# Two operand spacings in SBUF, for a fused attention and SwiGLU kernel: block words of h and the weights of 320 tokens

## The chip, the cores and the metric

One core of a Trainium2 chip runs the kernel. The metric is the device time of one execution in microseconds, lower is better. Before the change it is 702.36 us, the median of three runs (702.23 to 702.74).

## The reference

Attention is done in two steps through 32 packing tokens: the packing tokens p attend to k and v, and the queries then attend to what came out. The result, 4608 tokens by 512, goes through a gated feed-forward layer (512 to 1536 and back).

```python
def sm_attn(qq, kk, vv):
    s = scale * np.matmul(qq, kk.transpose(0, 1, 3, 2))
    a = np.exp(s - np.max(s, axis=-1, keepdims=True))
    a = a / (np.sum(a, axis=-1, keepdims=True) + 1e-09)
    return np.matmul(a, vv)
p_packed = sm_attn(p, k, v)              # 8 batches, 8 heads, 32 tokens, 64
out = sm_attn(q, p_packed, p_packed)     # 8 batches, 8 heads, 576 tokens, 64
x = out, as 4608 tokens by 512
g = x @ w_gate
return (g / (1 + np.exp(-g)) * (x @ w_val)) @ w_out
```

## The kernel before

Every float32 operand of a large product is split into two words, a high one that TensorE takes as it is and a low one that holds the rest, and a product is three matmuls: low by high, high by low, high by high.

The attention never forms its output. For each batch, m is the gate and value weights times the packed tokens (line 361, `m_mm`), and the gate and value of a chunk of h are m times the attention weights `a2` (line 1538 for batches 2 to 7, line 924 for batch 1, line 1104 for batch 0). In line 1538 the stationary operand is 128 columns of m and the moving one is `a2`, 320 tokens in a batch's first phase and 256 in its second. Each phase has 12 chunks, each chunk two sums (gate, value) and each sum six matmuls, so twelve matmuls of one width follow each other. ScalarE makes silu of the gate, VectorE multiplies (line 1552).

h times w_out goes by Strassen-like blocks (lines 1397 to 1407, `products`). GpSimd makes sums of h's blocks (`pair_sums`), and `pair_words` casts seven blocks of 128 columns to high words on ScalarE (line 1362) and takes the low words on VectorE (line 1363). In line 1404 these block words are stationary; the words of w_out or of sums of its blocks (`wo_h`, `wo_l`, `tA`, `tB`) are moving, 256 columns. A half of a pair has three block products, nine matmuls, the other half four, twelve matmuls.

`words_room` hands out two sets of rooms in turn. A set is a room for seven high words and one for seven low words, 896 elements of 4 bytes each. The first set lies in the second room of the ring `a2` (`x`), the second in a room called `pair9` (`y`) and behind the sums in `tB` (`z`):

```python
sums["set"] = ((x[:, 16:912], x[:, 1040:1936]), (y[:, 16:912], z[:, 16:912]))
```

All engines' queues follow orders written out by hand (`PROGRAM`, `FIRST`, `LATER` and the loops). `ROOMS` lists the SBUF rooms in the order in which they are laid out; sizes are rounded up to 32 bytes. Before the change the rooms of w_out's words, `tA`, `tB` and both rooms of `a2` start at 96 bytes modulo 256. The block words start 16 elements, 64 bytes, into rooms of that kind, so at 160. The rooms of m are at 160 as well: `mh` and `ml` start there, and those in `io0` and `io1` begin 16 elements in. All steps inside these operands that one matmul or the next takes are multiples of 256 bytes, or of 512 for stationary ones. So in lines 1538, 1404, 946, 924 and 1104 the stationary operand is 64 bytes (modulo 256) above the moving one throughout.

Of the kernel before, what the change touches and what calls it, by code (L numbers as in the profile page):

```python
# [11 lines left out]
F32R = mybir.dt.float32r  # L12
# [8 lines left out]
B, H, S, D = 8, 8, 576, 64  # L21
NP = 32
DM, DF = 512, 1536
P = 128
NPAR, NHP = 2, 4
NFC = DF // P
# [8 lines left out]
NA, NB = 256, 320  # L35
PART = slice(0, NA), slice(NA, NA + NB)
NZ = NA // P
PHASE = NB, NA
NT = B * S
SCALE = 1.0 / 8.0  # L40
POSITIVE_MOST = float(np.array(0x0FEFFFFF, np.int32).view(np.float32))
# [1 line left out]
LOW_WORD = 2.0**-29 * 15 / 16  # L43

ROOMS = (
    ("p", 512, 2), ("pp", 512, 1), ("ppt", 512, 2), ("z1", 64, 2),
    ("t2", 2560, 1), ("sg", 1280, 1), ("s2", 5120, 1), ("a1", 5120, 1), ("wA", 24576, 1), ("wB", 8192, 1), ("wC", 16384, 1),
    ("io0", 9216, 2), ("io1", 9216, 2), ("v", 10240, 1), *((f"pair{i}", 4096, 1) for i in range(NFC + 1)), ("a2", 9216, 2),
    ("t4", 6144, 1), ("hc", 8192, 1), ("nm1", 16, 2), ("hw", 6144, 1), ("ot", 5120, 1), ("x1", 256, 1), ("r2", 432, 1), ("mx1", 16, 2), ("mh", 4096, 2), ("ml", 4096, 2),
)  # L50

PROGRAM = """
# [108 lines left out]
def tile_pack_attention_swiglu(ctx: ExitStack, tc: tile.TileContext, q0, qT, qP, kT, kP, v, vq, pT, wgv, wout, out):  # L161
# [5 lines left out]
    pool = ctx.enter_context(tc.tile_pool(name="pool", bufs=1))  # L167
# [74 lines left out]
    rings, turns = {}, {}  # L242
# [62 lines left out]
    kps, vs, qs, st1, st2, a2, ppts = {}, {}, {}, {}, {}, {}, {}  # L305

    def piece(n):
        if "kqv" not in rings:
            rings["kqv"] = pool.tile([P, 2, 1280], F32, tag="v", bufs=1, name="kqv")
        return rings["kqv"][:, ring("kqv", 2), :n]  # L310
# [14 lines left out]
    def load_qp(b, i):  # L325
        n, at = PHASE[i], i * PHASE[0]
        x = piece(NHP * n)
        nc.sync.dma_start(x, qP[b - NEARLY, :, NHP * at : NHP * (at + n)])
        qs.setdefault(b, []).append(x.rearrange("p (h n) -> p h n", h=NHP))
# [272 lines left out]
    def s2_tiles(b):  # L602
        st2[b] = (
            pool.tile([P, 2, NPAR, HS] if b == 1 else [P, NPAR, S], F32, tag="s2", bufs=1, name="s2"),
            pool.tile([P, 3, 2 * NPAR * NBK], F32, tag="r2", bufs=1, name="r2"),
        )
# [172 lines left out]
    def y_tiles(b):  # L779
        s2_tiles(b)  # L780
        if "a2" not in rings:
            rings["a2"] = pool.tile([P, 2 * NPAR * S], F32R, tag="a2", bufs=2, name="a2")
        a2[b] = [
            [
                rings["a2"][:, at : at + NPAR * n].rearrange("p (r n) -> p r n", r=NPAR)
                for at in (2 * NPAR * PHASE[0] * i, 2 * NPAR * PHASE[0] * i + NPAR * n)
            ]
            for i, n in enumerate(PHASE)
        ]
# [9 lines left out]
    def y_flat(b, i):  # L799

        at = NPAR * PHASE[0]
        return st2[b][0].rearrange("p r n -> p (r n)")[:, slice(0, at) if i == 0 else slice(at, NPAR * S)]

    def y_view(b, i):

        n = PHASE[i]
        x = y_flat(b, i).rearrange("p (k n) -> p k n", n=NP)
        rows = slice(0, NPAR * PHASE[0] // NP) if i == 0 else slice(NPAR * PHASE[0] // NP, NPAR * S // NP)
        return x, [st2[b][1][:, j, rows] for j in range(3)], [P, NPAR * n // NP, NP]
# [89 lines left out]
    t4 = {}  # L899
# [54 lines left out]
    def emit_out(acc, row, eng):  # L954
# [21 lines left out]
        "pack": q_pack,  # L976
        "flip": q_flip,
        "tiles": y_tiles,
    }

# [22 lines left out]
    with tc.manual_schedule(engines={mybir.EngineType.PE}):  # L1003
# [17 lines left out]
        with tc.manual_schedule(  # L1021
# [190 lines left out]
            for word in PROGRAM.split():  # L1212
                name = word[: word.index(":") + 1] if ":" in word else word.rstrip("0123456789")
# [125 lines left out]
        sums = {"pairs": 0, "words": 0}  # L1339

        def words_room():

            i = sums["words"] % 2
            sums["words"] += 1
            if "set" not in sums:
                x = pool.tile([P, 2304], F32R, tag="a2", bufs=2, name="hw0")
                y = pool.tile([P, 1024], F32R, tag="pair9", bufs=1, name="hw1")
                z = t_tiles["B"][:, 3072:]
                sums["set"] = ((x[:, 16:912], x[:, 1040:1936]), (y[:, 16:912], z[:, 16:912]))
            return [x.rearrange("p (i n) -> p i n", n=P) for x in sums["set"][i]]  # L1350

        def pair_sums(x, eng=nc.gpsimd):
# [7 lines left out]
        def pair_words(x):  # L1360
            hi, lo = words_room()
            nc.scalar.copy(hi, x[:, 1:])  # L1362
            nc.vector.tensor_tensor(lo, x[:, 1:], hi.bitcast(F32), op=ALU.subtract)  # L1363
            return dict(zip(WORDS, ((hi[:, i], lo[:, i]) for i in range(7))))
# [14 lines left out]
        def rest_words(k, a22, tb, s):  # L1379

            hi, lo = words_room()
            srcs = ((slice(0, 2), tb[:, 2 * k : 2 * k + 2]), (2, a22), (slice(3, 7), s))
            for at, src in srcs:
                nc.scalar.copy(hi[:, at], src)
            for at, src in srcs:
                nc.vector.tensor_tensor(lo[:, at], src, hi[:, at].bitcast(F32), op=ALU.subtract)
            return dict(zip(("A11", "A12", "A22", *WORDS[3:]), ((hi[:, i], lo[:, i]) for i in range(7))))
# [127 lines left out]
        with tc.manual_schedule(  # L1515
# [3 lines left out]
            for b in range(2, B):  # L1519
                plan = plan_of(b)  # L1520
                for slot in range(2 * NFC):
                    ph, fc = divmod(slot, NFC)
                    k, f = divmod(fc, 2)
                    n, odd = PHASE[ph], b % 2
# [25 lines left out]
                    x = rings["hc"][:, sums["pairs"] % 2]  # L1550
# [106 lines left out]
```

## Time and profile before

| what | value |
|---|---|
| median of three runs | 702.36 us (702.23 to 702.74) |
| profiled execution | 702.56 us |
| its span, first to last instruction | 700.6 us |
| instructions | 16313 |
| TensorE busy | 694.6 us, 99% of the span |
| weight loads busy | 608.3 us, 87% |
| VectorE busy | 506.7 us, 72% |

The profiled execution is 2.0 us longer than its span: what lies around the first and the last instruction. Matmuls overlap in the profile (the next starts before the one ahead of it is recorded as ended), so a busy share of TensorE says little; the spacing from one start to the next does. The chain of work that ended last gives that: it is cut into pieces of one line, and a piece's length is the time from its start to the start of the next piece.

### The profile page before, as it was taken

The page shows a single profiled execution, that of the slowest core. Times are in us where ns is not written, and L with a number is a line of the kernel's source. Part 1 is how long each engine was busy: PE and PEld are TensorE (multiplying, and loading weights), DVE is VectorE, ACT ScalarE, POOL GpSimd, SP SyncE. Part 2 cuts the span into 40 slices and gives each one's busy share as a digit, 9 for nine tenths or more (in the row PEclk, how much of TensorE's full clock was granted, in tenths as well). Part 3 has the DMA queues.
Part 4 walks back from the last instruction along what each step waited for, and adds up shares of the span by engine and source line. Part 5 has one row for each costly group of instructions (what it writes and reads, how often), then busy time and mean ns, then how long its engine had stood idle before and what let it go on. Part 6 is the DMA issues. An engine that isn't in the chain of part 4 may idle for free.

```text
span 700.6 us, 16313 instructions
## 1 busy us (share of the span) xinstructions
PE 694.6 (99%) x6623; PEld 608.3 (87%) x6623; DVE 506.7 (72%) x1032; ACT 399.9 (57%) x670; POOL 167.2 (24%) x283
## 2 busy tenths in 40 slices
PE   9999999999999999999999999999999999999998
PEld 7777787887788988999988998899888998889997
DVE  4997997567886687757897559766687559753854
ACT  3999874655765457463375546745375546533432
POOL 0000005035162222123032222221231222223221
PEclk9999999999999999999999999999999999999999
DMA  9999942134263354513244416342544414320000
GB/s 348 363 341 342 356 183 99 45 107 151 71 229 109 112 167 150 192 64 133 82 165 139 154 69 219 127 162 64 185 156 142 153 69 155 107 109 1 31 31 31
DMA packets 27354, 103.53 MB, mean 148 GB/s; under 512 B 6800, under 2 KB 8336, under 8 KB 20112
## 3 DMA queue, kind: packets, MB, share of 16 engines
q1 hardware_dynamic: 26992, 102.30, 41.4%
q8 instruction: 52, 0.85, 0.5%
q10 hardware_dynamic: 288, 0.20, 0.1%
q14 instruction: 22, 0.18, 0.1%
HBM read 86.57 MB, written 15.91 MB: 146 GB/s over the span
## 4 chain that ended last, share of the span: by engine, by line
PE 88%; DMA 1%; DVE 0%; issue 0%
PE gv L1538 33%; PE acc L1404 30%; PE acc L946 8%; PE aux L361 8%; PE gv L924 5%; PE gv L1104 2%; PE aux L503 1%; PE aux L586 1%; DMA q_t<-in_qT 1%; PE end L1478 0%; DVE wo_f L227 0%; DVE ot L1487 0%; PE aux L598 0%; DVE wo_l L303 0%; DVE wo_f L226 0%; DVE hw L1137 0%
## 5 line engine op out<-in xcount | busy, mean ns | idle before, releaser
L1538 PE MATMUL gv<-a,m 128*128 128x320 f32 (+1 forms) x1728 | 251.0, 294 | 0.0
L1538 PEld LDWEIGHTS gv<-a,m 128*128 128x128 f32 x1728 | 232.0, 188 | 3.2 <-issue 2.3
L1548 ACT ACTIVATE sg<-gv 128x320 f32<-128x320 f32 (+1 forms) x144 | 59.3, 412 | 171.7 <-PE gv L1538 150.4
L1354 POOL TENSOR_TENSOR hc<-hc 128x256 f32<-128x256 f32 x69 | 51.1, 740 | 346.7 <-DVE hc L1552 346.7
L1552 DVE TENSOR_TENSOR hc<-gv,sg 128x256 f32<-128x256 f32 x144 | 60.3, 419 | 93.6 <-PE gv L1538 81.6
L1404 PE MATMUL acc<-wo_h,hw 128*128 128x256 f32 x500 | 125.6, 282 | 0.0
L1404 PEld LDWEIGHTS acc<-wo_h,hw 128*128 128x128 f32 x500 | 90.8, 188 | 11.0 <-issue 4.2
L1404 PE MATMUL acc<-wo_l,hw 128*128 128x256 f32 x332 | 92.5, 278 | 0.0
L1404 PE MATMUL acc<-tA,hw 128*128 128x256 f32 x420 | 75.0, 278 | 0.0
L1362 ACT CAST hw<-hc 128x896 fp32r<-128x896 f32 x71 | 66.5, 936 | 7.1 <-DVE hc L1358 3.9
L946 PE MATMUL acc<-wo_h,hw 128*128 128x512 f32 x192 | 69.7, 408 | 0.0
L1404 PEld LDWEIGHTS acc<-wo_l,hw 128*128 128x128 f32 x332 | 62.5, 188 | 0.0
L1404 PEld LDWEIGHTS acc<-tA,hw 128*128 128x128 f32 x420 | 60.8, 188 | 0.0
L946 PEld LDWEIGHTS acc<-wo_h,hw 128*128 128x128 f32 x192 | 36.1, 188 | 19.7 <-issue 11.3
L891 ACT CAST m<-aux 128x512 fp32r<-128x512 f32 x72 | 38.8, 592 | 23.1 <-PE aux L361 22.8
L849 DVE TENSOR_TENSOR m<-aux,m 128x512 fp32r<-128x512 f32 x72 | 46.0, 680 | 4.1 <-ACT m L891 4.0
L1404 PE MATMUL acc<-wo_h,tB 128*128 128x256 f32 x164 | 46.2, 282 | 0.0
L1363 DVE TENSOR_TENSOR hw<-hc,hw 128x896 fp32r<-128x896 f32 x36 | 39.3, 1091 | 7.0 <-ACT hw L1362 6.5
L1363 DVE TENSOR_TENSOR tB<-hc,hw 128x896 fp32r<-128x896 f32 x35 | 38.5, 1099 | 4.9 <-ACT hw L1362 4.5
L361 PE MATMUL aux<-wB,ppt 64*32 64x512 f32 x608 | 41.8, 601 | 0.0
L946 PE MATMUL acc<-wo_l,hw 128*128 128x512 f32 x96 | 38.0, 396 | 0.0
L1404 PE MATMUL acc<-tB,hw 128*128 128x256 f32 x204 | 36.8, 282 | 0.0
(240 smaller groups left out, 1195.7 us busy)
## 6 DMA issues: line engine op xcount, KB each, us to landing
wB<-wd SPq DMA_DIRECT2D x36, 1024.0 KB, 4.9
st<-in_wgv SPq DMA_DIRECT2D x12, 1024.0 KB, 7.9
out<-ot SPq DMA_DIRECT2D x33, 256.0 KB, 2.5
kqv<-in_vq SPq DMA_DIRECT2D x12, 640.0 KB, 4.1
kqv<-in_kP SPq DMA_DIRECT2D x12, 576.0 KB, 3.8
st<-in_wout SPq DMA_DIRECT2D x6, 1024.0 KB, 7.2
kqv<-in_qP SPq DMA_DIRECT2D x6, 640.0 KB, 4.5
wd<-wA SPq DMA_DIRECT2D x3, 1024.0 KB, 11.0
```

The source lines that it names most:

```text
L361: nc.tensor.matmul(outs[par][32 * hp : 32 * hp + 32], lhs(r, hp), rhs(r, hp), start=True, stop=True)
L849: pin(nc.vector.tensor_tensor(*lows.pop(0), op=ALU.subtract))
L891: nc.scalar.copy(m[0][at], src)
L924: nc.tensor.matmul(pg[:, :n], m_[:, g, f, s * P : (s + 1) * P], a_[:, g, off : off + n], start=(i == 0), stop=(i == 5),)
L946: nc.tensor.matmul(acc[:, :], h_[:, c : c + P], w_[fc // 2][:, fc % 2], start=(first and i == 0), stop=(fc == NFC - 1 and i == 2),)
L1354: eng.tensor_tensor(x[:, 4:6], x[:, 0].unsqueeze(1).broadcast_to([P, 2, P]), x[:, 1:3], op=ALU.subtract)
L1362: nc.scalar.copy(hi, x[:, 1:])
L1363: nc.vector.tensor_tensor(lo, x[:, 1:], hi.bitcast(F32), op=ALU.subtract)
L1404: nc.tensor.matmul(banks[bank][:, 256 * half : 256 * half + 256], s_, m_, start=(start and k == 0 and j == 0), stop=(k == last and j == 2 ...
L1538: nc.tensor.matmul(pg[:, :n], m_[:, g, f, s * P : (s + 1) * P], a_[:, g, :], start=(i == 0), stop=(i == 5))
L1548: nc.scalar.activation(sg[:, :n], pgs[0][:, :n], AF.Silu)
L1552: nc.vector.tensor_tensor(x[:, 2 * f : 2 * f + 2].rearrange("p i n -> p (i n)"), pgs[1][:, o : o + 256], sg[:, o : o + 256], op=ALU.mult,)
```

## The change

The two rooms of `a2` get 16 bytes more each (rounded up to 32), and inside the first, the weights of the 256 tokens come first and those of the 320 tokens behind them with a gap of 4 elements, 16 bytes. The list entry `nm1` (two rooms of 32 bytes) moves from behind `hc` to the front, so that everything from `t2` to `hc` starts 64 bytes later, and the 64 bytes that `a2` has grown by do the same for everything from `hw` on. The four rooms of block words start at other elements of the same tiles.

After it, modulo 256: w_out's words, `tA`, `tB` and the first room of `a2` at 160, m at 224. The 320 tokens' weights are at 176, 48 below m; the 256 tokens' at 160, 64 below m as before. The second room of `a2` starts at 192. The block words are at 32 (high) and 96 (low) above w_out's words in the first set and at 128 (high) and 160 (low) in the second.

```diff
+A2_AT = 2 * NPAR * NA + 4, 0
...
 ROOMS = (
-    ("p", 512, 2), ("pp", 512, 1), ("ppt", 512, 2), ("z1", 64, 2),
+    ("p", 512, 2), ("pp", 512, 1), ("ppt", 512, 2), ("z1", 64, 2), ("nm1", 16, 2),
...
-    ("io0", 9216, 2), ("io1", 9216, 2), ("v", 10240, 1), *((f"pair{i}", 4096, 1) for i in range(NFC + 1)), ("a2", 9216, 2),
-    ("t4", 6144, 1), ("hc", 8192, 1), ("nm1", 16, 2), ("hw", 6144, 1), ("ot", 5120, 1), ("x1", 256, 1), ("r2", 432, 1), ("mx1", 16, 2), ("mh", 4096, 2), ("ml", 4096, 2),
+    ("io0", 9216, 2), ("io1", 9216, 2), ("v", 10240, 1), *((f"pair{i}", 4096, 1) for i in range(NFC + 1)), ("a2", 9232, 2),
+    ("t4", 6144, 1), ("hc", 8192, 1), ("hw", 6144, 1), ("ot", 5120, 1), ("x1", 256, 1), ("r2", 432, 1), ("mx1", 16, 2), ("mh", 4096, 2), ("ml", 4096, 2),
...
-            rings["a2"] = pool.tile([P, 2 * NPAR * S], F32R, tag="a2", bufs=2, name="a2")
+            rings["a2"] = pool.tile([P, 2 * NPAR * S + 4], F32R, tag="a2", bufs=2, name="a2")
...
-                for at in (2 * NPAR * PHASE[0] * i, 2 * NPAR * PHASE[0] * i + NPAR * n)
+                for at in (A2_AT[i], A2_AT[i] + NPAR * n)
...
-                sums["set"] = ((x[:, 16:912], x[:, 1040:1936]), (y[:, 16:912], z[:, 16:912]))
+                sums["set"] = ((x[:, 0:896], x[:, 1040:1936]), (y[:, 32:928], z[:, 40:936]))
```

## Rows read from the trace of the kernel before

**Rows 1.** The page's first part: engine, busy us, share of the span, instructions.
```profile
span 700.6 us, 16313 instructions
PE 694.6 (99%) x6623; PEld 608.3 (87%) x6623; DVE 506.7 (72%) x1032; ACT 399.9 (57%) x670; POOL 167.2 (24%) x283
```
**Rows 2.** The page's chain that ended last: shares by engine and by line.
```profile
PE 88%; DMA 1%; DVE 0%; issue 0%
PE gv L1538 33%; PE acc L1404 30%; PE acc L946 8%; PE aux L361 8%; PE gv L924 5%; PE gv L1104 2%; PE aux L503 1%; PE aux L586 1%; DMA q_t<-in_qT 1%; PE end L1478 0%; DVE wo_f L227 0%; DVE ot L1487 0%; PE aux L598 0%; DVE wo_l L303 0%; DVE wo_f L226 0%; DVE hw L1137 0%
```
**Rows 3.** Waits of the weight loads: waiting line, releaser, us in total, times, longest.
```profile
PEld acc L1404 <- DVE tB L1363: 4.2, 5, 0.8
```
**Rows 4.** The chain in order, 198 to 300 us: start us, us, line, matmuls.
```profile
213.32 1.75 PE gv L1538 x12
215.08 1.37 PE acc L1404 x12
218.20 1.03 PE acc L1404 x9
...
228.15 1.41 PE acc L1404 x12
...
231.32 1.06 PE acc L1404 x9
...
245.16 1.36 PE gv L1538 x12
...
247.22 1.57 PE acc L1404 x12
...
250.15 1.02 PE aux L361 x16
...
272.99 1.62 PE acc L1404 x12
274.61 1.41 PE gv L1538 x12
```
**Rows 5.** The chain in order, 600 us to the end.
```profile
604.39 1.36 PE gv L1538 x12
...
622.93 1.37 PE acc L1404 x12
...
626.06 1.03 PE acc L1404 x9
...
643.46 1.76 PE gv L1538 x12
...
654.40 14.84 PE acc L1404 x126
...
686.62 1.06 PE acc L1404 x9
...
689.09 1.41 PE acc L1404 x12
690.51 1.41 PE gv L1538 x12
```
**Rows 6.** The chain over the whole span, among its longest pieces.
```profile
327.79 14.70 PE acc L1404 x126
```
**Rows 7.** Timeline, 300 to 303 us: start us, us, engine, line, matmuls or loads.
```profile
302.34 0.28 PE L1404 MATMUL acc<-wo_h,hw 128*128 128x256 f32 x1
302.34 0.73 PEld L1538 LDWEIGHTS gv<-a,m 128*128 128x128 f32 x5
302.45 0.74 PE L1538 MATMUL gv<-a,m 128*128 128x320 f32 x4
```
**Rows 8.** Groups by line and shape: busy us, mean ns of one.
```profile
L1538 PE MATMUL gv<-a,m 128*128 128x320 f32 x864 | 138.5, 309 | 0.0
```
**Rows 9.** Line 1404 alone over the span: busy us and instructions, granted clock.
```profile
0.00:700.60 700.60, 230.58 (x1743) 213.68 (x1743) 1.00 0.42 148
```

## The prediction

> **What bounds the kernel now.** I read the first part of the page first: TensorE is busy 694.6 us of a 700.6 us span, and the next engine, VectorE, has 72% [rows 1]. Then the chain that ended last: 88% of it is TensorE, two thirds of that the two lines that the change touches, the gate and value products (line 1538) and the products with w_out (line 1404) [rows 2]. Then the waits in front of the weight loads: the largest releaser with a name, VectorE's line 1363, costs 4.2 us in the whole run, so nobody keeps TensorE waiting for long [rows 3]. What is left to gain or lose is the spacing of back-to-back matmuls, so I read the chain's pieces (how long 9, 12 or more matmuls of one line took, from their first to the next piece's first).
>
> The pieces come in two levels. Twelve matmuls of 256 columns take 1.36 us in one place and 1.41 us in another, nine take 1.02 or 1.06 us: 113.3 or 117.5 ns for one [rows 4, 5]. Line 1538 and line 1404 share these levels, and a level, once there, lasts over several pieces: from 646 us to the end nearly every piece of 256 columns is at 1.41 or 1.06 [rows 5]. Of the pieces of twelve without a start-up in line 1404, 29 are at 1.36 or 1.37 and 16 at 1.41 or 1.42; of nine, 22 at 1.02 or 1.03 and 20 at 1.05 or 1.06; in line 1538 with 256 columns, 38 at 1.36 and 22 at 1.41 or 1.42. With 320 columns there is no such choice: all 68 separate pieces of twelve, first to last, are at 1.75 or 1.76 us, 146.5 ns for one [rows 4, 5]. At the quick level's time per column they would take 1.36 x 320/256 = 1.70 us. The bytes read are alike in all of them, and the operands stand 64 bytes apart (modulo 256) everywhere; so one spacing of the operands allows both levels, and the trace holds no other spacing for these two lines.
>
> Why spacing could matter at all is seen in the timeline: the weight load of a matmul starts as the matmul before it starts (302.34 us for both), so stationary words of the next and moving words of the present one are fetched from SBUF at the same time [rows 7].
>
> **The change part by part.** No instruction, transfer, wait or queue position is added, removed or moved, so no engine's count changes and SP's queue stays as it is. Two spacings change on purpose, (a) and (b), and two more with them, (c).
>
> (a) The 320-token weights: 864 matmuls, 72 groups of twelve [rows 8]. Their moving operand now ends up 48 bytes (modulo 256) below the stationary one, 64 before. No row has this spacing, so the price has to be bounded. Below: they come to the quick level, 72 x (1.757 - 1.70) = 4.1 us gained. Above: they lose one more step of the size that separates the two levels, 146.5 x 117.5/113.3 = 151.9 ns, 864 x 5.4 ns = 4.7 us lost. The nearest rows are the two levels of the 256 columns [rows 4, 5]: there 64 bytes allow the quick level, while with 320 columns they never do, whichever level the pieces in front have (215.08 to 231.32 us has both). A loss that is there in all of 68 pieces is of the kind that a fixed spacing can cause, and I take the lower end: 4.1 us gained.
>
> (b) The block words of h: 1743 matmuls of 256 columns [rows 9], 64 bytes from w_out's before, then 32 and 96 in one set, 128 and 160 in the other. Bounds again from the two levels. If every piece went to the quick level: 16 x 0.05 + 20 x 0.04 for the plain pieces, 6 x 0.04 for pieces of twelve with a start-up (1.61 or 1.62, against 1.57 or 1.58 of 16 others), and 14.70 + 14.84 - 2 x 126 x 0.1133 = 0.99 for the two runs of 126: 2.8 us gained [rows 4 to 6]. Since the level carries over into line 1538's 256-column groups, whose own spacing stays at 64, these would follow: 22 x 0.05, 1.1 us more. If every piece went to the slow level: 29 x 0.05 + 22 x 0.04 + 16 x 0.04 + 0.14 = 3.1 us lost, and 38 x 0.05 = 1.9 us with line 1538. A level worse than 1.41 is not excluded; one more step of 4.2 ns would be 7.3 us on 1743 matmuls. Four different spacings will hardly all be good or all be bad, and at one spacing both levels occur already. So I take the middle, nothing, and keep both ends.
>
> (c) The rooms move as a whole by 64 bytes against the few that stay below them (p, ppt, z1). This shifts the stationary ppt against the gate and value words in line 361, which is 8% of the chain, 56 us [rows 2]. One level step of 3.7% there would be 2.1 us to either side. The 32 pieces in which its 16 matmuls stand alone and entire take 1.02 us each [rows 4], so it shows no second level: nothing. The second room of a2 ends up 32 bytes further on than the rest, so batch 1's weights, which lie there, come to 32 bytes from the words of line 924, 64 before; that line is 5% of the chain, 35 us, and a step 1.3 us. Nothing again, as in (b), and 3.4 us to either side for both.
>
> (d) VectorE, ScalarE and GpSimd read and write the same shapes at other addresses. VectorE, the busiest of them, has 28% idle time [rows 1], which would cover a step of 4%; without that cover it would show as longer waits of the weight loads, now 4.2 us behind line 1363 [rows 3]. A quicker TensorE meets these waits a little sooner; a few tenths of a us.
>
> Sum: 4.1 us off 702.56 us, the time of the profiled execution (span 700.6 and 2.0 around it), is 698.5 us; against the median of 702.36 us, 0.2 lower, it is 698.3 us.
>
> The Trainium skill speaks against all of this (SBUF — State Buffer, "SBUF: two separate sides"): among engines only the port pair that VectorE and GpSimd share makes anyone wait, and TensorE has ports of its own for moving and stationary operands. By that rule the sum is zero, 702.4 us. The trace agrees so far as no row names another engine as the cause of the two levels, but it shows two levels, which the rule doesn't explain; so it stays a rival, below. The skill's gap of N / 2.4 + 2.5 ns (TensorE: Matmul & The Clock Gate, "Back-to-back issue gap") would give 109.2 ns for 256 columns and 135.8 ns for 320; no stretch of this trace reaches either.
>
> **The rivals.**
> R1, no difference: the two levels come from when a group starts, not from where its operands stand. For it: one spacing shows both levels, and a level persists across lines with different tiles [rows 4, 5]. Against it: the 320s never leave theirs. Time 702.4 us.
>
> R2, slower: the new spacings of the block words are worse than 64. One of every three stationary loads in line 1404 takes low words and two take high words, so a bad spacing in one room touches a sixth or a third of 1743 matmuls; all rooms at the slow level and line 1538 with them cost 3.1 + 1.9 = 5.0 us. With the 320s unchanged and the products alone slow: 705.5 us. It decides against my forecast when the products lose more than the 4.1 us of (a): 2.4 ns a matmul, over half of the step of 4.2 ns. For it: 64 already keeps more than half of the pieces at the quick level, so a blind move has more to lose than to win.
>
> R3, both gain: the 320s at 1.70, all else at 1.36 and 1.02: 4.1 + 2.8 + 1.1 = 8.0 us, 694.4 us. For it: products behind a 320-column group are at 1.37 where they are quick, not 1.36 [rows 4, 5], and a quick 320 would hand on a quick start. Against it: level changes also follow the stalls at line 361, which stay.
>
> R4, the gain of (a) and a loss in (b) of 3.1 us nearly cancel: 701.4 us.
>
> **How the numbers follow.** Forecast 0.36 (own range 696.2 to 700.4, the 2.1 us of line 361), R3 0.13, R1 0.17, R2 0.27, R4 0.07. A measurement of this kernel tells 0.2%, 1.4 us, from no change. Faster: forecast and R3, with a hundredth of R1: 0.50. Same: R1 and most of R4: 0.22. Slower: R2 and a hundredth of R4: 0.28. For 8 in 10 the range reaches from below R3, 693.0 us, to 706.5 us, which is R2 with half of what line 1538 can add; what loses both ways, up to 702.4 + 5.0 + 4.7 = 712.1 us, stays outside.
>
> **What the next profile would show.** (a) is right if the 320-column pieces of twelve stand near 1.70 us, and wrong at 1.75 or above. (b) is right if pieces of 1.36 and 1.41 are about as many as now; R2 shows as pieces at 1.41 or more where both words come from one set, with the other set quick; R3 as no 1.41 left. (c) is right if line 361's pieces stay at 1.02. R1 shows as the same levels in the same proportion. Wrong altogether would be a change in instruction counts, in the granted clock, now 1.00 [rows 9], or a new releaser of the weight loads.

## The result, and the profile after

The change made the kernel slower: 710.64 us against 702.30 us (four runs each, 710.11 to 711.82 against 702.05 to 702.74), a ratio of 1.0117 (interval 1.0102 to 1.0132). The profiled execution took 711.82 us, with a span of 709.8 us, 9.2 us more than before.

The first part of the page (engine, busy us, share of the span, instructions), and the chain's shares by engine:

```profile
span 709.8 us, 16313 instructions
PE 703.0 (99%) x6623; PEld 616.6 (87%) x6623; DVE 507.2 (71%) x1032; ACT 398.7 (56%) x670; POOL 166.8 (23%) x283
...
PE 95%; DMA 2%; DVE 1%; ACT 1%; issue 0%; SPq 0%; ACTq 0%; DVEq 0%
```

Every count is as in [rows 1]; TensorE and its weight loads each have some 8 us more, the other engines are within 1.2 us of before. So TensorE's own instructions became longer, at the same granted clock. Line 1404, now 1405, alone over the span (busy and instructions of matmuls, then of weight loads; then the granted clock):

```profile
0.00:709.80 709.80, 234.18 (x1743) 217.20 (x1743) 1.00 0.42 146
```

Against [rows 9] that is 3.6 us more for the same 1743 matmuls. The waits of the weight loads have not grown: the largest with a name is still 4.2 us, as in [rows 3] (as many times and as long, put down to another of VectorE's instructions):

```profile
PEld acc L1405 <- DVE a L843: 4.2, 5, 0.8
```

The chain in order of time, 198 to 300 us (start us, us, line, matmuls; all lines of the kernel are one higher than before):

```profile
217.90 1.76 PE gv L1539 x12
219.66 1.06 PE acc L1405 x9
220.73 1.83 PE gv L1539 x12
222.55 1.42 PE acc L1405 x12
223.97 1.83 PE gv L1539 x12
225.80 1.02 PE aux L362 x16
...
245.99 1.07 PE acc L1405 x9
247.05 1.41 PE gv L1539 x12
...
249.16 1.61 PE acc L1405 x12
...
254.46 1.38 PE gv L1539 x12
```

And 600 us to the end:

```profile
643.42 1.83 PE gv L1539 x12
645.25 1.42 PE acc L1405 x12
...
655.63 1.37 PE gv L1539 x12
657.00 1.42 PE acc L1405 x12
...
663.69 14.88 PE acc L1405 x126
```

Three things differ from [rows 4, 5]. The products (line 1405) have lost the quick level: from 198 us on, 44 pieces of twelve stand at 1.41 or 1.42 and none at 1.36, 46 of nine at 1.06 or 1.07 and none at 1.02. The 256-column groups of line 1539 stand mostly at 1.41 or 1.42, 53 of 62, where it was 22 of 62. And the 320-column groups, which had one level, now have two: 33 pieces at 1.75 or 1.76 and 35 at 1.82 or 1.83. The pieces of line 362 still take 1.02 us.

Where the 9.2 us went follows from each matmul's interval to the start of the next one, summed by line and width in both traces:

| line before, columns | change, us |
|---|---|
| 1404, 256 | +3.5 |
| 1538, 320 | +2.7 |
| 1538, 256 | +1.9 |
| 361, 512 | +0.6 |
| 924, 256 | +0.6 |
| all else, no row more than 0.4 either way | -0.1 |

### The profile page after: what moved, and what is told of

Its sections match the earlier page's. It is cut to its first block, busy times and chain, and to the rows that moved or that the text cites. A ratio compares the mean times of both kernels' runs of the same rounds, so it can differ in the third digit from the quotient of the medians.

```text
span 709.8 us, 16313 instructions
## 1 busy us (share of the span) xinstructions
PE 703.0 (99%) x6623; PEld 616.6 (87%) x6623; DVE 507.2 (71%) x1032; ACT 398.7 (56%) x670; POOL 166.8 (23%) x283
## 4 chain that ended last, share of the span: by engine, by line
PE 95%; DMA 2%; DVE 1%; ACT 1%; issue 0%; SPq 0%; ACTq 0%; DVEq 0%
PE gv L1539 32%; PE acc L1405 30%; PE acc L947 9%; PE aux L362 8%; PE gv L925 5%; PE gv L1105 5%; DMA st<-in_wgv 1%; PE aux L587 1%; PE aux L504 1%; DMA k_t<-in_kT 1%; DMA out<-ot 1%; PE warm_ps L1009 1%; PE end L1479 0%; PE acc_aux L684 0%; PE aux L444 0%; PE acc_aux L362 0%
## 5 line engine op out<-in xcount | busy, mean ns | idle before, releaser
L1539 PE MATMUL gv<-a,m 128*128 128x320 f32 (+1 forms) x1728 | 255.5, 297 | 0.2 <-ACT sg L1549 0.2
L1539 PEld LDWEIGHTS gv<-a,m 128*128 128x128 f32 x1728 | 236.1, 189 | 3.4 <-issue 2.3
```

The source lines that it names most:

```text
L1539: nc.tensor.matmul(pg[:, :n], m_[:, g, f, s * P : (s + 1) * P], a_[:, g, :], start=(i == 0), stop=(i == 5))
```

## The experiments

Three questions were open: which edit costs what; whether the spacing of the two operands decides, or where one of them starts, or how a group begins; and which spacings are good. "Spacing" is the stationary operand's address minus the moving one's, modulo 256, throughout. Each kernel was compared with the kernel before in runs on the same chip.

**words_only**: the kernel before with the block words alone moved, to spacings 32, 96, 128 and 160.

```diff
-                sums["set"] = ((x[:, 16:912], x[:, 1040:1936]), (y[:, 16:912], z[:, 16:912]))
+                sums["set"] = ((x[:, 8:904], x[:, 1048:1944]), (y[:, 32:928], z[:, 40:936]))
```

> Of the change only the block words move: 32 and 96 bytes (modulo 256) from w_out's words in the first set, 128 and 160 in the second; attention weights and all rooms stay as before. Theory A (the spacing of a matmul's stationary operand from its moving one sets its pace): line 1404 loses its quick level as it did in the changed kernel, 3.5 us, and line 1538's 256 columns lose it with them, 1.9 us; the 320 columns stay at 1.76 us for twelve: 707.7 us, 5.4 over 702.3. Theory B (the levels come from when groups start, and the spacing does not matter): 702.3 us, pieces of 1.36 and 1.41 in the old proportion. Theory C (the rooms' 64-byte shift against p, ppt and z1 did it): 702.3 us as well.

Measured: 707.78 us against 701.85, ratio 1.0091 (1.0077 to 1.0105). Its chain from 400 to 440 us, and below it its line 1404 alone over the span:

```profile
401.39 1.76 PE gv L1538 x12
403.15 1.42 PE acc L1404 x12
...
406.33 1.06 PE acc L1404 x9
...
420.23 1.36 PE gv L1538 x12
...
428.91 1.42 PE acc L1404 x12
```
```profile
0.00:705.70 705.70, 234.20 (x1743) 216.97 (x1743) 1.00 0.42 147
```

The products lose all that they lose in the full change (234.20 us busy against 234.18). By intervals line 1404 costs 3.6 us and line 1538's 256-column groups, none of whose addresses moved, 1.7 us: a slow level is handed on. The 320-column pieces keep 1.76.

**weights_only**: all of the change except the words, which go back to a spacing of 64.

```diff
-                sums["set"] = ((x[:, 0:896], x[:, 1040:1936]), (y[:, 32:928], z[:, 40:936]))
+                sums["set"] = ((x[:, 8:904], x[:, 1032:1928]), (y[:, 16:912], z[:, 16:912]))
```

> All of the change but the block words, which stay 64 bytes from w_out's words. Theory A: the 320-token weights at 48 bytes lose 2.7 us as in the changed kernel, line 924 at 32 bytes 0.6 us, line 361 0.6 us, and line 1404 keeps both its levels: 706.2 us, 3.9 over 702.3; line 1538's 256 columns keep pieces of 1.36. If words and weights add, this and the words-only run make 8.3 to 9.3 us together. Theory B: 702.3 us. Theory C: nearly the whole loss is here, above 708 us, and line 1404 is slow although its spacing is 64.

Measured: 705.97 us against 701.85, ratio 1.0055 (1.0043 to 1.0068). Its chain from 400 to 440 us, and its groups by line and shape (busy us, mean ns of one):

```profile
400.37 1.83 PE gv L1539 x12
402.20 1.37 PE acc L1405 x12
403.57 1.83 PE gv L1539 x12
...
437.77 1.02 PE acc L1405 x9
```
```profile
L1539 PE MATMUL gv<-a,m 128*128 128x320 f32 x864 | 143.7, 315 | 0.0
```

The 320-column matmuls took 138.5 us before [rows 8] and take 143.7 here. By intervals that is 5.1 us lost: 745 of 842 stand at 153 to 154 ns, from one start to the next. The products, at 64 again, gain 2.0 us and the 256-column groups 0.9, since nearly all of them are quick here.

**rooms_only** and **rooms_32**: the kernel before with a gap of 64, or of 32, bytes ahead of `t2`. With 64 the stationary `ppt` moves against line 361's words as it does in the change; with 32 all large operands move together by half of that. All other spacings stay.

```diff
-    ("p", 512, 2), ("pp", 512, 1), ("ppt", 512, 2), ("z1", 64, 2),
+    ("p", 512, 2), ("pp", 512, 1), ("ppt", 512, 2), ("z1", 64, 2), ("gap", 64, 1),
```

> Only a gap of 64 bytes in front of t2: every room behind z1 starts 64 bytes later, so all spacings stay but those of ppt and p to the gate and value words and to k and q (lines 361 and 503). Theory A: line 361 may lose up to 0.6 us, nothing else moves: 702.3 to 702.9 us. Theory B: 702.3 us. Theory C: 706 us or more, with line 1404 and line 1538 at the slow level.

> The kernel before with a gap of 32 bytes in front of t2: all spacings of lines 1404 and 1538 stay at 64, but each moving operand starts at 128 modulo 256, a multiple of 64, where it started at 32 past one. Theory A: as before, 701.9 us, twelve of 320 columns in 1.76 us. Theory D with steps of 32 bytes: the same 701.9 us. Theory D with steps of 64 bytes: the 320 columns come to 1.70 us or near it: 698 us or less.

Measured: 701.62 us against 701.85, ratio 0.9997 (0.9988 to 1.0006), and 702.70 against 702.65, ratio 1.0001 (0.9993 to 1.0010). Neither line 361's spacing nor where the operands start as a whole makes a difference that can be measured.

**m_map_a, m_map_b, m_map_c**: the kernel before with four of the six rooms of m (k = 0 to 3, named `ma` to `md`) each at a spacing of its own; the other two, named `m`, stay at 64. The lists are (0, 32, 48, 96), (16, 80, 128, 160) and (112, 144, 192, 224).

```diff
+M_AT = (0, 32, 48, 96)
...
-                t = pool.tile([P, 2304], F32R, tag=f"io{k // 2}", bufs=2, name="m")
+                t = pool.tile([P, 2304], F32R, tag=f"io{k // 2}", bufs=2, name=("ma", "mb", "mc", "md")[k])
+                o = M_AT[k] // 4
...
-                    t[:, at : at + 4 * 2 * P].rearrange("p (r f n) -> p r f n", r=NPAR, f=2) for at in (16, 16 + 8 * P)
+                    t[:, at : at + 4 * 2 * P].rearrange("p (r f n) -> p r f n", r=NPAR, f=2) for at in (o, o + 8 * P)
```

> The kernel before, with the four rooms of m in io0 and io1 at 0, 32, 48 and 96 bytes (modulo 256) above the attention weights in place of 64; the other two rooms of m stay at 64, as do the block words. One run thus shows line 1538 at five spacings, with 320 and with 256 columns. Theory A: the rooms differ from each other in a fixed way; at 64 the 256 columns have a median duration of 276 to 278 ns, at 32 and 96 some 280 or more as line 1404 had in the changed kernel; the 320 columns at 48 are some 3 ns over those at 64; 0, where both operands meet the same place, is the slowest of the five. Theory B: all five have the same median within 1 ns, and the whole is 702.3 us.

> The kernel before, with the four rooms of m at 16, 80, 128 and 160 bytes above the attention weights, two rooms at 64 as control. Theory A for 256 columns (64 is a good spacing, its neighbours are not): each of the four at 117 ns or more, the control at 114 ns, as 0, 32, 48 and 96 had been (119.6, 118.4, 117.9, 120.2 against 114.1). 320 columns: 146.6 to 147.1 ns at each, as at 0 to 96, with the weights at 96. Together some 705 us. Theory B (starts, not spacing): no room differs from the control by more than 1 ns.

> The kernel before, with the four rooms of m at 112, 144, 192 and 224 bytes above the attention weights, two rooms at 64 as control. If spacing counts modulo 256, one or more of these may be as good as 64; if it counts modulo 128, 192 is like 64 (114 ns with 256 columns) and 224 like 96 (120 ns). 320 columns: 146.6 to 147.1 ns throughout, as at 0 to 96. Theory B: no room differs from the control by more than 1 ns.

Measured: 705.33 us against 701.85, ratio 1.0050 (1.0032 to 1.0069); 705.21 against 702.65, ratio 1.0036 (1.0021 to 1.0051); 701.78 against 702.65, ratio 0.9989 (0.9979 to 0.9999). Each room is a row of the groups by shape (busy us, mean ns of one; that mean runs to a matmul's end, so it is some 163 ns longer than the interval between starts). m_map_a:

```profile
L1540 PE MATMUL gv<-a,m 128*128 128x256 f32 x288 | 36.8, 277 | 0.0
...
L1540 PE MATMUL gv<-a,md 128*128 128x256 f32 x144 | 19.3, 283 | 0.0
L1540 PE MATMUL gv<-a,mb 128*128 128x256 f32 x144 | 19.0, 282 | 0.0
```

m_map_b:

```profile
L1540 PE MATMUL gv<-a,m 128*128 128x256 f32 x288 | 36.8, 277 | 0.0
...
L1540 PE MATMUL gv<-a,md 128*128 128x256 f32 x144 | 19.2, 282 | 0.0
L1540 PE MATMUL gv<-a,mb 128*128 128x256 f32 x144 | 19.0, 282 | 0.0
```

m_map_c:

```profile
L1540 PE MATMUL gv<-a,m 128*128 128x320 f32 x288 | 46.1, 309 | 0.0
...
L1540 PE MATMUL gv<-a,md 128*128 128x320 f32 x144 | 23.1, 308 | 0.0
...
L1540 PE MATMUL gv<-a,ma 128*128 128x256 f32 x144 | 20.2, 290 | 0.0
L1540 PE MATMUL gv<-a,mb 128*128 128x256 f32 x144 | 19.1, 282 | 0.0
L1540 PE MATMUL gv<-a,mc 128*128 128x256 f32 x144 | 18.9, 280 | 0.0
L1540 PE MATMUL gv<-a,md 128*128 128x256 f32 x144 | 18.7, 279 | 0.0
```

A room's row is to be compared with the same room of another kernel, since `ma` and `mc` have more groups that begin after a stall. `md` has 283 ns at 96 and 282 at 160; `mb` has 282 at 32, 80 and 144. At the good spacings of two later kernels (both_16, m_192) both have 276 or 277, in a third (both_192) `md` has 277 and `mb` 279. `mc` has 285 at 48 and 128, and 280 at 192; `ma` has 289, 288 and 290 at 0, 16 and 112, and 285 or 286 in those three. From one start to the next within a room's pieces, long waits left out, the 256-column matmuls take on the mean:

| spacing, bytes | ns between starts |
|---|---|
| 64 (rooms k = 4, 5 of the three kernels) | 114.1, 114.1, 113.5 |
| 192 | 113.7 |
| 224 | 116.6 |
| 0, 16, 32, 48, 80, 96, 112, 128, 144, 160 | 117.9 to 120.6 |

The pieces of twelve that hold no wait say it more plainly. In the three maps, at 64 and 192 most take 1.36 us and the others 1.41, at 224 all take 1.40, and at the ten other spacings they take 1.41 to 1.44, none less. Where an operand starts is not what decides here. The weights start at the same place in all three maps. The stationary operand of m_map_b's room at 128 starts at the same place (modulo 256) as the rooms of m in rooms_only, whose 256-column matmuls, at a spacing of 64, keep the quick level (1.36 or 1.37 in 53 of 62 pieces).

With 320 columns the same rooms stand between 146.5 and 147.9 ns whatever the spacing: here no spacing helps, and none of these costs much. The 3 ns that were expected at 48 did not come (146.9 ns against 146.8 at 64).

**both_16**: weights_only with the 256 tokens' weights 16 bytes on as well, so that both stand at 176, and `ma` to `md` moved after them to restore 64; `m` is left at 48. The rooms take their starts from the list as in the maps. It asks whether the moving operand's start at 176 is the cause by itself.

```diff
-A2_AT = 2 * NPAR * NA + 4, 0
+A2_AT = 2 * NPAR * NA + 4, 4
...
+M_AT = (80, 80, 80, 80)
```

> As the run that had all of the change but the block words, with the 256-token weights and four of the six rooms of m 16 bytes later as well. So attention weights start at 176 modulo 256 with both widths; four rooms of m stand 64 bytes above them, the last two 48. In the m-map run 48 bytes cost the 320 columns nothing (146.9 ns, weights at 96), in the weights-only run they took 152.7 ns (weights at 176). Theory D (the moving operand's own start is what counts for 320 columns: 16 bytes past a multiple of 32 is slow): 320 columns at 152 to 153 ns from all six rooms, the one at 64 as the one at 48; the 256 columns lose their quick level too: 707 to 709 us. Theory A (spacing): 320 columns at 146.6 ns from the four rooms at 64 and at 153 from the two at 48, pieces of twelve at 1.76 and 1.83 us, 256 columns at 113.3 ns from four rooms: 704 us.

Measured: 705.72 us against 702.65, ratio 1.0050 (1.0035 to 1.0066). Its groups by shape:

```profile
L1541 PE MATMUL gv<-a,m 128*128 128x320 f32 x288 | 46.6, 311 | 0.0
...
L1541 PE MATMUL gv<-a,m 128*128 128x256 f32 x288 | 38.1, 282 | 0.0
...
L1541 PE MATMUL gv<-a,md 128*128 128x320 f32 x144 | 23.0, 308 | 0.0
...
L1541 PE MATMUL gv<-a,md 128*128 128x256 f32 x144 | 18.5, 277 | 0.0
L1541 PE MATMUL gv<-a,mb 128*128 128x256 f32 x144 | 18.5, 277 | 0.0
```

With the spacing of 64 restored, none of the 320-column matmuls stands at 153 ns. Left at 48, some do: 53 of 287 at 153 to 154 ns, and 282 with 256 columns. So the start alone falls as a cause of the 153 ns level. The 256-column matmuls of the restored rooms did not come to the 113.3 ns that were expected: they take 115.0 to 116.7 ns, since their pieces begin with several slower matmuls before the rest go at 113 or 114 (1.38 us for twelve). Whether that is the start or the slow groups in front of them was not tested.

**m_all_48**: the kernel before with `ma` to `md` all at 48 and the weights where they were, at 96.

```diff
+M_AT = (48, 48, 48, 48)
```

> The kernel before with four of the six rooms of m at 48 bytes above the attention weights (two stay at 64); the weights start at 96 modulo 256 as before. So 320 columns run at the changed kernel's spacing, but with the 16 bytes taken from the stationary side: m starts 16 past a multiple of 32, the weights do not. Theory A (spacing alone): groups of 320 columns in two levels, 1.76 and 1.83 us for twelve, the second in at least a third of the groups from these four rooms; 706 us or more. Theory E (it takes the spacing of 48 and the moving operand 16 bytes past a multiple of 32): every group at 1.75 to 1.77, as from the one room at 48 in the first m-map run; 256 columns at 117 to 118 ns from the four rooms; 705 us.

Measured: 704.63 us against 702.08, ratio 1.0033 (1.0021 to 1.0046). The 256-column matmuls are slow (118.0 ns between starts), but the 320-column ones stay at 146.8 and no group shows 153. So the 153 ns level was seen only with both: a spacing of 48, and weights that start 16 bytes past a multiple of 32.

**words_192, m_192, both_192**: the kernel before with the other good spacing, for the block words, for `ma` to `md` (their starts from the list as in the maps), and for both.

```diff
-                sums["set"] = ((x[:, 16:912], x[:, 1040:1936]), (y[:, 16:912], z[:, 16:912]))
+                sums["set"] = ((x[:, 48:944], x[:, 1072:1968]), (y[:, 48:944], z[:, 48:944]))
...
+M_AT = (192, 192, 192, 192)
```

> The kernel before with all block words 192 bytes (modulo 256) from w_out's words in place of 64. Theory A with a period of 128 bytes: line 1404 keeps its quick level, pieces of 1.36 and 1.02 us as well as some of 1.41 and 1.06: 702.3 us or up to 4 less, and not 707.8 as at 32, 96, 128 and 160. A period of 256, with 192 good for line 1538 by chance: 706 to 708 us. Theory B: 702.3 us.

> The kernel before with the four rooms of m in io0 and io1 at 192 bytes above the attention weights in place of 64, two rooms at 64, block words at 64. Theory A with a period of 128: 256 columns at 113.3 to 114 ns from all six rooms, 320 at 146.5, line 1404 as before or a little better, as in the third m-map run (701.8 us with three of four rooms at other spacings): 699 to 702 us. Theory B: 702.3 us.

> The two before together: block words and four rooms of m at 192. Theory A with a period of 128: the sum of the two, 697 to 702 us; if which level a group takes is settled by how it starts, the number of pieces at 1.41 and 1.06 differs from run to run of these three while none goes above. Theory B: 702.3 us.

Measured: 701.65 us, ratio 0.9994 (0.9985 to 1.0003); **699.69 us, ratio 0.9969 (0.9956 to 0.9981)**; 702.70 us, ratio 1.0011 (1.0003 to 1.0020); all against 702.08. m_192 is quicker than both kernels of the case. The chain of m_192, 620 to 700 us, its line 1406 alone (1404 before) over the span, and its groups by shape:

```profile
647.03 1.36 PE gv L1540 x12
...
652.13 14.67 PE acc L1406 x126
...
673.76 1.02 PE acc L1406 x9
...
676.14 1.36 PE acc L1406 x12
```
```profile
0.00:697.70 697.70, 228.74 (x1743) 211.81 (x1743) 1.00 0.42 148
```
```profile
L1540 PE MATMUL gv<-a,md 128*128 128x256 f32 x144 | 18.3, 276 | 0.0
L1540 PE MATMUL gv<-a,mb 128*128 128x256 f32 x144 | 18.3, 276 | 0.0
```

Here the stretch from 647 us to the end, nearly all slow before [rows 5], is quick, and line 1406 is 1.8 us shorter than [rows 9], though no address of its own moved. Yet both_192, with both pairs at 192, came out above the 702 us that it was given at most: it has 32 product pieces of twelve at 1.41 or 1.42, and `ma` and `mb` stand there at 117.8 ns, where `mb` had 113.3 in m_192 at the same spacing. Its row of the groups by shape:

```profile
L1540 PE MATMUL gv<-a,mb 128*128 128x256 f32 x144 | 18.9, 279 | 0.0
```

A good spacing allows the quick level and does not bring it about; how the groups in front leave TensorE has a part in it that these runs do not resolve.

## Why the prediction was wrong, point by point

**The step that failed first is (a), by its sign.** It took 4.1 us as gained; the 320-column matmuls lost 2.7 us in the change and 5.1 us by themselves (weights_only), a little over the upper bound of 4.7 (151.9 ns was taken, 153 to 154 measured). By the prediction's own sign, pieces of twelve at 1.75 or above, (a) is wrong. The reasoning was that a loss seen in all 68 pieces is what a fixed spacing would cause, so another spacing would cure it. The map says otherwise: at 64 and at twelve other spacings the 320 columns stand at 146.2 to 147.9 ns. A cost that is there at the only spacing in the trace is no evidence that spacing causes it. The one way in which spacing showed here was for the worse.

**Step (b) was mis-sized.** It took the middle of its bounds, nothing, on the ground that four new spacings would hardly all be bad. All four are: the words at 32, 96, 128 and 160 have 117.8 to 118.7 ns each in the trace of after, against 115.7 on the mean before. Line 1404 lost 3.5 us, 0.4 more than the bound of 3.1 (all pieces at the slow level), and the carry-over to line 1538's 256-column groups, priced at up to 1.9 us, came out at 1.9 (1.7 in words_only). The assumption that failed is that 64 was a spacing like any other. Of twelve others tried only 192 matches it, and 224 comes halfway.

**Step (c)** held for line 361: the same shift alone is worth nothing (rooms_only), and its pieces keep 1.02 us; the 0.6 us that it has more in this pair of profiles was not traced further (in weights_only, with the same shift, it has 0.3 us less). Line 924 lost 0.6 us, within the 1.3 us kept for it: batch 1's 256 tokens are at 32, one of the slow spacings. **Step (d)** held: the waits of the weight loads have not grown.

**The rivals.** R1, no difference, is refuted. So, here, is the zero that the prediction drew from the rule beside it, of the Trainium skill (SBUF — State Buffer, "SBUF: two separate sides"), that among engines only the port pair shared by VectorE and GpSimd causes contention: no row names another engine, yet moving one operand of TensorE against the other costs up to 7 ns a matmul (120.6 against 113.5 in m_map_c); the measurement decides. That both operands are fetched from SBUF at the same time was the prediction's reason why spacing could matter; no run shows what makes a spacing good or bad. R2 had the mechanism of the words right, the point that 64 has more to lose than to win too, and its 5.0 us are 5.4 measured by line. It left the 320 columns unchanged. R3 and R4 needed the gain of (a) and fall with it. The case that came true is R2 with a loss in (a), which the prediction had named and left outside its range, with 712.1 us.

**The sum.** By the medians the two halves alone cost 5.9 and 4.1 us, together 10.0, and the change 8.3. By the spans of the profiled executions it is the other way: 5.1 and 2.1 us, together 7.2, and the change 9.2. The profile of weights_only is that of its fastest run (704.75 us) and that of the change of its slowest (711.82 us), so whether the two halves add up is not shown. What the lines do show is that the halves act on each other: with the words slow, only about half of the 320-column groups go to 153 ns, 2.7 us where it was 5.1, and the products and the 256 columns forgo the 2.9 us that they gain in weights_only. Why the 320-column groups choose their level so, and why slow ones leave quick products behind them in weights_only, stays open.

## What to carry to other kernels

Where TensorE runs back to back and loads new weights for each matmul, lay the moving and the stationary operands out on purpose and measure the spacing between them: here, with 256 columns, 64 and 192 bytes were good and eleven others cost 3 to 7 ns of 113. Before moving a layout, count how much of the quick level it already has; one that shows it may be at one of few good places, and a blind move has more to lose than to gain. Price such a change by pieces of the chain, not by instruction counts, and include the neighbours, since a level is handed on to groups whose own addresses never moved.

## What the runs showed that was not expected

- The two good spacings lie 128 bytes apart: 64 and 192 have 113.5 to 114.1 ns in the three maps, but 0 and 128, the other multiples of 64, are slow (119.6 and 118.4 ns).
- The matmuls of 320 columns are indifferent to the spacing, except that a spacing of 48 with weights that start at 176 gave them a level of 153 ns that no other kernel showed. With the weights at 176 and a spacing of 64 it was absent, with a spacing of 48 and the weights at 96 too.
- At a good spacing two levels live side by side, 113.3 and 117.5 ns, and a change that leaves all spacings of the large products alone can shift how often each occurs: of line 1538's 61 or 62 pieces of twelve with 256 columns and no wait, 53 took 1.36 or 1.37 us in rooms_only, 34 in rooms_32 and 38 in the kernel before. The kernel before took from 700.67 to 703.73 us in one set of 24 runs; that this comes from the two levels is not shown, since only one execution of it was profiled.
